# Feed-forward: the rank of the first product's groups, floored to pairs

## The chip, the cores and the metric

The kernel runs on one core of a Trainium2 chip. The metric is the device time of one execution in microseconds (us); the shown time is the median of three runs. Beside it stands one profiled execution, from which all rows below are taken. In the text PE is TensorE (matrix products), PEld its weight loads, DVE VectorE, ACT ScalarE, POOL GpSimd, and SP SyncE, which here only issues DMAs.

## The reference

Hashed attention, then a feed-forward block. Of the attention only this matters here: its output, laid out as `x` with 3072 tokens of 512 features, feeds the block. The block is

```
h = x @ w_in                                              # 3072 x 512 by 512 x 2048
g = h * erf(softplus(h))
y = g @ w_out                                             # 3072 x 2048 by 2048 x 512
```

all in float32 on the chip.

## The kernel before

**Stages.** The attention takes about the first 312 us. Then comes `feed_forward`, the function that the change touches. It works on six tiles of 512 tokens, t = 0 to 5.

**The first product** (`x @ w_in`) of tiles 1 to 5 is done by Winograd's form of Strassen's method at two levels. The outer level makes seven products of half-size blocks, in the order `CHAIN` = P1, P6, P2, P7, P4, P5, P3 (line 1455). Each of them is split once more into seven *groups* in the order `INNER` = Q1, Q5, Q6, Q2, Q7, Q3, Q4 (line 1633). So a tile has 49 groups. A group (`small`, line 1660) is four float32 matmuls of 128x128 by 128x128, which the profile shows as eight MATMUL rows at L1672. Tile 0 has one level only (`plain`, L1433).

**The second product** (`g @ w_out`) is seven products M1 to M7 of eight pieces each (`project`, L1989, four MATMUL rows a piece, 128x256). From the third tile on (t = 2) M4, M7 and M3 are split a second time: seven quarter-block groups in place of eight pieces (`project_small`, L2145, eight MATMUL rows). While tile t runs its first product, the second product of tile t-1 runs beside it; after tile 5's first product only second products are left. The last tile keeps M3 in pieces.

**Accumulators.** A group writes one PSUM bank (`where_of`, L1656): Q1, Q6, Q7 and Q4 share M1 or M2, by turns from one outer product to the next; Q2 uses M4; Q5 and Q3 use M5. After Q1 its bank is copied into M4 by ACT (`seed`, L1449), and Q2 adds to that copy. After each of the other six groups the bank is added to or copied into the hidden block in SBUF (`add_small`: DVE L1702, ACT L1699). The next group of the same bank has to wait for that read. In INNER the groups of the shared bank stand two places apart.

**Weights.** The blocks of `w_in` and their precomputed sums lie in DRAM and come through a ring of two buffers: `load_wi` (L1641, issued by SP) loads the seven operands of an outer product when the outer product two before it has run its last group. The sums of `x` (`presum_xi`, L1654) are made by POOL.

**The gate.** Each hidden block of 128x1024 is put through six ACT instructions (L1821 once, L1829 four times, L1846 once) and three DVE instructions (L1835 twice, L1850 once), which alternate. Sums of gated blocks for the second product are DVE's (L1908 and, for quarter blocks, L2120). The last of them for the last tile stand ahead of M5 and M6 of that tile.

**Who sets the order.** Nothing of this order is written out by hand. Every step is an `Op` with a name, an engine, a cost, a rank, the steps that it comes after, and the ring room it takes. `by_need` (L187) plays the engines against each other with the costs and writes one order for each. On PE the step with the lowest `(rank, name)` is taken among those that could start at that moment (`place`, L240). On the other engines it is the step that is due first, where due times are counted back from PE's order. It plays 5 rounds for each of 3 margins and keeps the order whose PE ends first. The engines then follow that order, and semaphores hold them where a step is late.

The two products are two chains on PE, "P" and "M" (`pe`, L1388): within one, each step comes after the one before, so the rank decides only how the two are interleaved. The ranks before: group g of outer product i of tile t has

```
rank = (0, t + (i + g / 7) / 7)
```

that is, t + (7i + g)/49. A piece or quarter group of the second product of tile t-1 has t + 0.04 + n/56, where n counts the steps in the script (53 a tile with quarter blocks, 56 without). The step of the first is 1/49 = 0.0204, of the second 1/56 = 0.0179.

Of the kernel before, what the change touches and what calls it, by code (L numbers as in the profile page):

```python
# [294 lines left out]
def kernel(  # L295
# [1045 lines left out]
    def feed_forward(pools, check, late):  # L1341
# [27 lines left out]
        def op(name, engine, cost, rank, fn, args, reads=(), writes=(), after=(), **more):  # L1369

            needs = set(after)
            for x in tuple(reads) + tuple(writes):
                if x in wrote:
                    needs.add(wrote[x])
            for x in writes:
                needs |= read.get(x, set())
            for x in reads:
                read.setdefault(x, set()).add(name)
            for x in writes:
                wrote[x] = name  # L1380
                read[x] = set()
            needs.discard(name)
            more.setdefault("late", dict(PE=0.4, DVE=0.3, ACT=0.3, POOL=0.35, SP=0.3)[engine])
            ops.append(
                Op(name, engine, cost, rank, lambda: fn(*args), after=tuple(sorted(needs, key=str)), **more)
            )

        def pe(chain, name, cost, rank, fn, args, **more):  # L1388
            after = more.pop("after", ())
            if last[chain]:  # L1390
                after += (last[chain],)
            last[chain] = name
            op(name, "PE", cost, rank, fn, args, after=after, **more)
# [4 lines left out]
        def part(t, q, fl, tl=None):  # L1398
            room = homes[t][q]
            if tl is None:  # L1400
                return tuple(("h", room, fl, n) for n in range(2))
            return (("h", room, fl, tl),)
# [5 lines left out]
        def xkey(t, name):  # L1408
            key = XKEY[name]
            return key + (t % 2,) if key[0] == "x" else key  # L1410
# [226 lines left out]
        def number(t, i):  # L1637
            return (t if again else t - 1) * 7 + i
# [17 lines left out]
        def where_of(t, i, q):  # L1656
            n = number(t, i) % 2
            return (("M1", "M2")[n]) if q in ("Q1", "Q6", "Q7", "Q4") else dict(Q2="M4").get(q, "M5")
# [23 lines left out]
        def seeded(t, i):  # L1682
            return number(t, i) > 0

        def fresh_of(t, i, q):
            return q in ("Q2" if seeded(t, i) else "Q1", "Q6", "Q5", "Q4")
# [24 lines left out]
        def load_ops(t, i):  # L1711
            n = number(t, i)
            op(
                ("load_wi", t, i),
                "SP",
                0.1,
                (1, t + (i - 1.6) / 7, 0),
                load_wi,
                (t, i),
                reads=(("wi", CHAIN[i], 0), ("wi", CHAIN[i], 1)),  # L1720
                writes=(("ring", n % 2),)
                + (tuple(("w", name, n) for name in ("P1", "P2", "P4", "P7")) if n < 2 else ()),
                late=12.0 if (t, i) == (1, 0) else 8.5,
                far=True,
            )

        def chain_ops(t):
            for i, name in enumerate(CHAIN):
                n = number(t, i)
                into, base = TARGET[name]  # L1730
                load_ops(t, i)
                op(
                    ("presum_xi", t, i),
                    "POOL",
                    1.9,
                    (1, t + (i - 1.5) / 7 if t > 1 or i > 2 else (0.55, 0.6, 0.9)[i], 1),
                    presum_xi,
                    (t, i),
                    writes=(xkey(t, name), ("inn", n % 3)),
                    port=True,  # L1740
                )
                for g, q in enumerate(INNER):
                    rank = (0, t + (i + g / 7) / 7)
                    where = where_of(t, i, q)
                    fl, tl = dict(
                        Q1=(0, 0), Q2=(0, 0), Q6=(0, 1), Q3=(0, 1), Q5=(1, 1), Q7=(1, 1), Q4=(1, 0)
                    )[q]
                    pe(
                        "P",
                        ("small", t, i, q),  # L1750
                        0.875,
                        rank,
                        small,
                        (t, i, q),
                        reads=(xkey(t, name), ("inn", n % 3), ("ring", n % 2)),
                        writes=(("bank", where),),
                    )
                    if q == "Q1" and seeded(t, i):
                        op(
                            ("seed", t, i),  # L1760
                            "ACT",
                            0.51,
                            rank,
                            seed,
                            (where, "M4"),
                            reads=(("bank", where),),
                            writes=(("bank", "M4"),),
                        )
                        continue
                    fresh = fresh_of(t, i, q)  # L1770
                    copy = fresh and base is None
                    target = (("s2", fl, tl),) if into is None else part(t, into, fl, tl)
                    op(
                        ("add_small", t, i, q),
                        "ACT" if copy else "DVE",
                        0.51 if copy else 0.61,
                        rank,
                        add_small,
                        (t, i, q),
                        reads=(("bank", where),) + (part(t, base, fl, tl) if fresh and base is not None else ()),  # L1780
                        writes=target,
                    )
                if name == "P5":
                    for fl in range(2):
                        both = (("s2", fl, 0), ("s2", fl, 1))
                        op(
                            ("add_far", t, fl),
                            "POOL",
                            0.87,
                            (0, t + 6 / 7, fl),  # L1790
                            add_far,
                            (t, fl),
                            reads=both,
                            writes=part(t, 3, fl),
                            late=7.0,
                            far=True,
                        )
                        op(
                            ("add_both", t, fl),
                            "DVE",  # L1800
                            1.16,
                            (0, t + 6 / 7, fl),
                            add_both,
                            (t, fl),
                            reads=both,
                            writes=part(t, 1, fl),
                            port=True,
                        )
# [601 lines left out]
        if again:  # L2410
            load_x(0)
            for k in range(4):
                presum_x(0, k)
            chain_ops(0)
        else:
            if late:
                for k in range(3, 7):
                    name = ("P5", "P6", "P7", "P3")[k - 3]
                    reads = {4: (("w", "P5", 1),), 6: (("w", "P6", 1),)}.get(k, ())
                    op(  # L2420
                        ("late", k), "DVE", 1.16, (1, 0.2, k), late, (k,), port=True,
                        reads=reads, writes=(("w", name, 1),), after=(("late", k - 1) if k > 3 else ("complete", 0, 0),),
                    )
            plain_ops()
            inner_ops()
            presum_w_ops()
        for q in (0, 2, 3, 1):
            gate_ops(0, q)
        for t in range(1, NTILE + 1):
            rest = second_ops(t - 1)  # L2430
            if t < NTILE:
                x_ops(t)
                chain_ops(t)
                for q in (0, 2, 3, 1):
                    gate_ops(t, q)
            rest()
# [143 lines left out]
```

## Time and profile before

| | us |
|---|---|
| median of 3 runs (lowest, highest) | 873.22 (872.52, 875.36) |
| the profiled execution, its own time | 873.12 |
| its span, first to last instruction | 871.3 |
| PE busy | 864.3 |
| DVE busy | 748.9 |
| ACT busy | 638.3 |
| first group of tile 1 starts | 365.24 |
| last group of tile 5 starts | 812.51 |
| last instruction of PE ends | 866.87 |

All times in rows are us from the start of the span; a mean or a minimum in ns is marked. A timeline row gives start, length, engine, line, operation, what is written and read, the shape, and the number of instructions merged in it; in brackets is the idle time of that engine just before, and what ended it. A MATMUL row's length runs past the start of the next one, since matmuls are pipelined: what a group costs PE is the distance from its start to the start of the next. A row cut by the edge of a window shows fewer instructions.

Two facts of the code help in reading it: the output of all groups of the first product reads `M<-area,w_in_sb` or `M<-i,w_in_sb` at L1672; the second product's pieces read `w_out_sb` or `wt` at L1989; quarter groups are at L2145.

### The profile page before, as it was taken

The page shows a single profiled execution, that of the slowest core. Times are in us where ns is not written, and L with a number is a line of the kernel's source. Part 1 is how long each engine was busy: PE and PEld are TensorE (multiplying, and loading weights), DVE is VectorE, ACT ScalarE, POOL GpSimd, SP SyncE. Part 2 cuts the span into 40 slices and gives each one's busy share as a digit, 9 for nine tenths or more (in the row PEclk, how much of TensorE's full clock was granted, in tenths as well). Part 3 has the DMA queues.
Part 4 walks back from the last instruction along what each step waited for, and adds up shares of the span by engine and source line. Part 5 has one row for each costly group of instructions (what it writes and reads, how often), then busy time and mean ns, then how long its engine had stood idle before and what let it go on. Part 6 is the DMA issues. An engine that isn't in the chain of part 4 may idle for free.

```text
span 871.3 us, 15275 instructions
## 1 busy us (share of the span) xinstructions
PE 864.3 (99%) x5992; PEld 671.1 (77%) x5992; DVE 748.9 (86%) x926; ACT 638.3 (73%) x895; POOL 210.5 (24%) x274
## 2 busy tenths in 40 slices
PE   9999999999999999999999999999999999999997
PEld 5444544444454468898999999999999999999997
DVE  5999999999899799789996877699779979898982
ACT  6888888887888757796589457845777586858840
POOL 1111111111111000425241453226632433210000
PEclk9999999999999999999999999999999999999999
DMA  9566866556662246685564647545486657655311
GB/s 223 153 183 193 221 196 181 174 148 171 180 176 103 87 158 219 219 316 203 191 167 162 228 136 226 180 153 201 132 274 235 205 146 229 219 170 164 102 63 41
DMA packets 99825, 155.30 MB, mean 178 GB/s; under 512 B 35182, under 2 KB 48542, under 8 KB 98848
## 3 DMA queue, kind: packets, MB, share of 16 engines
q1 hardware_dynamic: 90112, 120.96, 44.6%
q0 software_dynamic: 9184, 32.81, 12.4%
q8 instruction: 49, 0.80, 0.4%
q10 hardware_dynamic: 448, 0.46, 0.2%
q14 instruction: 32, 0.26, 0.1%
HBM read 119.50 MB, written 29.46 MB: 171 GB/s over the span
## 4 chain that ended last, share of the span: by engine, by line
PE 96%; DVE 1%; DMA 1%; ACT 1%; issue 0%; DVEq 0%
PE M L1672 24%; PE M L1989 23%; PE st L687 18%; PE av L772 15%; PE M L1433 6%; PE M L2145 5%; PE X L2145 3%; PE bits L975 1%; DMA w_in_sb<-wi_P 1%; PE bits L816 1%; PE warm L936 1%; DVE area L1908 0%; PE X L1989 0%; DVE h L1850 0%; DVE e L1835 0%
## 5 line engine op out<-in xcount | busy, mean ns | idle before, releaser
L687 PE MATMUL st<-q,k 64*128 64x384 f32 x768 | 155.1, 482 | 0.0
L1672 PE MATMUL M<-area,w_in_sb 128*128 128x128 f32 x1120 | 146.6, 275 | 1.4 <-DVE h L1702 1.2
L1672 PEld LDWEIGHTS M<-area,w_in_sb 128*128 128x128 f32 x1120 | 142.2, 192 | 6.4 <-DVE h L1702 1.6
L1835 DVE SCALAR_TENSOR_TENSOR e<-w,e 128x1024 f32<-128x1024 f32 x96 | 125.1, 1303 | 19.8 <-ACT w L1829 19.5
L1702 DVE TENSOR_TENSOR h<-M,h 128x512 f32<-128x512 f32 x161 | 108.4, 685 | 33.2 <-PE M L1672 29.3
L1989 PE MATMUL M<-w_out_sb,h 128*128 128x256 f32 x528 | 130.7, 380 | 0.0
L1829 ACT ACTIVATE w<-h,cq 128x1024 f32<-128x1024 f32 x96 | 109.7, 1142 | 22.1 <-DVE e L1835 22.1
L1829 ACT ACTIVATE w<-w,cq 128x1024 f32<-128x1024 f32 x96 | 110.3, 1149 | 1.8
L1672 PEld LDWEIGHTS M<-i,w_in_sb 128*128 128x128 f32 x840 | 107.9, 192 | 3.9
L1672 PE MATMUL M<-i,w_in_sb 128*128 128x128 f32 x840 | 110.4, 275 | 0.0
L1989 PEld LDWEIGHTS M<-w_out_sb,h 128*128 128x128 f32 x528 | 92.8, 191 | 8.5
L1989 PE MATMUL M<-wt,area 128*128 128x256 f32 x384 | 96.3, 380 | 0.0
L687 PEld LDWEIGHTS st<-q,k 64*128 64x128 f32 x768 | 68.5, 187 | 35.8 <-issue 34.4
L760 DVE TENSOR_TENSOR area<-area 128x1536 f32<-128x1536 f32 (+1 forms) x46 | 79.2, 1721 | 6.9 <-ACT area L714 5.7
L1654 POOL TENSOR_TENSOR i<-area,i 128x128 f32<-128x128 f32 x70 | 46.3, 682 | 139.2 <-PE M L1672 138.2
L1821 ACT ACTIVATE e<-h,cq 128x1024 f32<-128x1024 f32 x48 | 54.9, 1145 | 33.8 <-DVE h L1702 22.0
L714 ACT ACTIVATE e_even<-st 128x768 f32<-128x768 f32 x96 | 73.9, 819 | 0.4 <-PE st L687 0.3
L714 ACT ACTIVATE area<-st 128x768 f32<-128x768 f32 x90 | 72.7, 811 | 0.3 <-PE st L687 0.3
L1989 PEld LDWEIGHTS M<-wt,area 128*128 128x128 f32 x384 | 66.9, 191 | 6.0 <-DVE area L1908 0.2
L1850 DVE TENSOR_TENSOR h<-h,e 128x1024 f32<-128x1024 f32 x48 | 61.0, 1270 | 9.5 <-ACT e L1846 9.4
L772 PE MATMUL av<-e_even,v 128*64 128x385 f32 x384 | 65.7, 490 | 0.0
L687 PE MATMUL st<-both 64*128 64x384 bf16 x384 | 63.0, 323 | 0.2 <-ACT e_even L714 0.2
(187 smaller groups left out, 1325.4 us busy)
## 6 DMA issues: line engine op xcount, KB each, us to landing
w_in_sb<-wi_P SPq DMA_DIRECT2D x35, 1792.0 KB
raw<-in_w_out_dram POOLq DMA_DIRECT2D x16, 512.0 KB, 4.3
raw<-in_w_in_dram POOLq DMA_DIRECT2D x14, 512.0 KB, 5.6
v<-in_v_dram SPq DMA_DIRECT2D x32, 192.0 KB
out_dram<-area SPq DMA_DIRECT2D x23, 256.0 KB
q<-in_qkT_dram SPq DMA_DIRECT2D x30, 192.0 KB
k<-in_qkT_dram SPq DMA_DIRECT2D x30, 192.0 KB
r<-rd SPq DMA_DIRECT2D x30, 192.0 KB
```

The lines of the kernel that those rows point to most:

```text
L687: nc.tensor.matmul(out=st[:, ab, 0:HS], lhsT=d["k" + src][rows, keys], rhs=d["q" + src][rows, cols], start=(part == 0), stop=(part == 1),)
L714: nc.scalar.activation(out=e[:, :, 0:HS], in_=st[:, :, 0:HS], func=AF.Exp, scale=scale)
L760: nc.vector.tensor_tensor(out=into, in0=one, in1=two, op=ALU.add)
L772: nc.tensor.matmul(out=d["av", half][rows, 0:w], lhsT=d["v"][:, g * GC + c, rows], rhs=e[:, ab, 0:w], start=(g == 0 and c == 0), stop=(g = ...
L1672: nc.tensor.matmul(out=out_[:, c, :], lhsT=ring[:, W_AT[q], n % 2, c * P : (c + 1) * P], rhs=x, start=((q in ("Q1", "Q5") or q == "Q2" and ...
L1702: nc.vector.tensor_tensor(out=out_, in0=bank_, in1=one, op=ALU.add)
L1821: nc.scalar.activation(out=s, in_=unit(t, q, fl), func=AF.Sigmoid, bias=cq[:, 0:1])
L1829: nc.scalar.activation(out=st["q", t, q, fl, j], in_=f, func=func, scale=scale, bias=cq[:, column : column + 1])
L1835: nc.vector.scalar_tensor_tensor(out=s, in0=st.pop(("q", t, q, fl, j)), scalar=GATE_S[j][1], in1=s, op0=ALU.add, op1=ALU.mult,)
L1850: nc.vector.tensor_tensor(out=h, in0=h, in1=st.pop(("s", t, q, fl)), op=ALU.mult)
L1989: nc.tensor.matmul(out=where[:, sub, :], lhsT=a[:, j // G, j % G, sub * P : (sub + 1) * P], rhs=b[:, j, :], start=first, stop=end, skip_gr ...
L2145: nc.tensor.matmul(out=where[:, n * P : n * P + P], lhsT=a[:, j, :], rhs=b[:, j, :], start=(q in ("Q1", "Q2") and j == 0), stop=(q in ("Q4 ...
```

## The change

One line: the position of the group within the tile, 7i + g, is rounded down to an even number before it becomes the rank.

```
 for g, q in enumerate(INNER):
-    rank = (0, t + (i + g / 7) / 7)
+    rank = (0, t + (7 * i + g - (7 * i + g) % 2) / 49)
     where = where_of(t, i, q)
```

So positions 0 and 1 share a rank, 2 and 3, and so on; position 48, the last of a tile, stands alone. The same rank goes to the group's reader (`seed` or `add_small`), where it counts only after the due time. No step is added or removed, no bank, cost, shape or dependency is altered, and the order within the P chain and within the M chain stays as it is. What changes is the interleaving of the two chains on PE, and through the due times the order that `by_need` writes for DVE, ACT, POOL and SP. An outer product with even i starts a pair with Q1: (Q1 Q5)(Q6 Q2)(Q7 Q3)(Q4, and Q1 of the next). One with odd i starts within a pair: Q1 there, then (Q5 Q6)(Q2 Q7)(Q3 Q4).

## Prediction

> **What bounds the kernel now.** I read the page first, then PE's waits, then the busy times by stage. The page and the waits:
>
> ```profile
> span 871.3 us, 15275 instructions
> ...
> PE 864.3 (99%) x5992; PEld 671.1 (77%) x5992; DVE 748.9 (86%) x926; ACT 638.3 (73%) x895; POOL 210.5 (24%) x274
> ```
> ```profile
> engine line waited for: us in total, times, longest us
> PE M L1672 <- DVE h L1702: 1.2, 1, 1.2
> PE warm L936 <- DVE ones L351: 1.0, 1, 1.0
> PE M L1672 <- DMA w_in_sb<-wi_P: 0.2, 1, 0.2
> PE st L687 <- ACT e_even L714: 0.2, 1, 0.2
> ```
>
> PE is busy for 864.3 of 871.3 us, and in the whole span it waits four times. Two of these waits lie in the stage that the change touches, both ahead of a group of the first product (L1672). A busy PE need not be a fast one, so the distances between starts count more than the 99%. By stage, one window for each of tiles 1 to 5 of the first product:
>
> ```profile
> core 0: us, PE busy (x) PEld busy (x) DVE busy (x) ACT busy (x) POOL busy (x), PEclk, DMA share, GB/s
> 365.00:454.00 89.00, 87.80 (x595) 82.08 (x595) 79.11 (x84) 67.16 (x73) 35.56 (x41) 1.00 0.67 229
> 454.00:546.00 92.00, 92.00 (x618) 86.23 (x617) 70.59 (x73) 63.70 (x71) 34.08 (x40) 1.00 0.56 183
> 546.00:638.00 92.00, 92.00 (x696) 88.39 (x695) 75.47 (x83) 58.22 (x73) 43.43 (x46) 1.00 0.56 178
> 638.00:729.00 91.00, 91.00 (x698) 87.70 (x698) 79.85 (x95) 65.27 (x81) 30.85 (x34) 1.00 0.65 211
> 729.00:814.00 85.00, 84.76 (x637) 81.22 (x636) 73.40 (x90) 66.22 (x79) 13.20 (x20) 1.00 0.57 184
> ```
>
> PE idles 1.20 us in the first window and 0.24 us in the last, nowhere else; its clock is granted in full (1.00) in all five. DVE is the next engine, 79.11 of 89 us (89%) in the first window and 79.85 of 91 (88%) in the fourth. What the steps cost PE is read from PE's timeline:
>
> ```profile
> 560.11 1.05 PE L1672 MATMUL M<-area,w_in_sb 128*128 128x128 f32 x8
> 561.00 1.03 PE L1989 MATMUL M<-w_out_sb,h 128*128 128x256 f32 x4
> 561.87 1.05 PE L1672 MATMUL M<-i,w_in_sb 128*128 128x128 f32 x8
> 562.76 1.03 PE L1989 MATMUL M<-w_out_sb,h 128*128 128x256 f32 x4
> 563.62 1.05 PE L1672 MATMUL M<-i,w_in_sb 128*128 128x128 f32 x8
> 564.52 1.06 PE L1672 MATMUL M<-area,w_in_sb 128*128 128x128 f32 x8
> ```
>
> A group of the first product (P) costs 0.89 us from its start to the next start, whether a piece of the second (M) follows (560.11 to 561.00) or another group (563.62 to 564.52: 0.90). A piece costs 0.86 to 0.87. So PE works at one pace whatever the interleaving, and only its waits can move.
>
> **What the change does to PE's pace.** The same groups and pieces run, in another mixture: mostly P P M M where it was P M P M. A pair's ranks lie 2/49 = 0.0408 apart, the M steps 1/56 = 0.0179, so 2.29 of them fall between two pairs: two, and every third or fourth time three. The rows above already hold both neighbourhoods, and they differ by 0.01 us at most, the last digit shown. There are 245 groups:
>
> ```profile
> L1672 PE MATMUL M<-area,w_in_sb 128*128 128x128 f32 x1120 | 146.6, 275 | 1.4 <-DVE h L1702 1.2
> ...
> L1672 PE MATMUL M<-i,w_in_sb 128*128 128x128 f32 x840 | 110.4, 275 | 0.0
> ```
>
> (1120 + 840)/8 = 245, so at most 122 new neighbourhoods, and 122 x 0.01 bounds the term at -1.2 to +1.2 us. I take 0, because the digit rounds either way.
>
> **What it does to the waits for readers.** The groups of the shared bank (Q1, Q6, Q7, Q4) stand two places apart in P. Before, Q6 M Q2 M Q7: 0.89 + 2 x 0.865 = 2.62 us of other work between Q6's end of issue and Q7. After, an even outer product gives Q6 Q2 M M Q7, an odd one Q6 M M Q2 Q7: the same 2.62 us. With a group's length of 1.05 and its pace of 0.89 the reader has 0.89 + 2.62 - 1.05 = 2.46 us. Two distances shrink from five steps to four, 3.5 us, and stay the longer ones: Q1 to Q2 in an even outer product (through the seed), and Q3 to the next Q5 from an odd to an even one. So no reader is given a shorter time than the shortest of before. What is new is that readers come in twos, 0.89 us apart, and then not for 2.6. In an odd outer product the first of the pair (Q5, Q2, Q3) is not urgent and the second (Q6, Q7, Q4) is; if the first goes first, the second starts later by one add. An add, and the wait that the trace has:
>
> ```profile
> 406.99 1.36 DVE L1908 TENSOR_TENSOR area<-h,h 128x1024 f32<-128x1024 f32 x1
> 408.28 1.48 DVE L1908 TENSOR_TENSOR h<-h,h 128x1024 f32<-128x1024 f32 x1
> 409.86 0.69 DVE L1702 TENSOR_TENSOR h<-M,h 128x512 f32<-128x512 f32 x1
> ```
> ```profile
> 405.71 3.69 PE L1989 MATMUL M<-wt,area 128*128 128x256 f32 x16
> 410.60 1.16 PE L1672 MATMUL M<-area,w_in_sb 128*128 128x128 f32 x8 [1.20 <-DVE h L1702]
> 411.74 2.86 PE L1989 MATMUL M<-wt,area 128*128 128x256 f32 x12
> 414.43 0.83 PE L1672 MATMUL M<-area,w_in_sb 128*128 128x128 f32 x6
> ```
>
> The add takes 0.69 us, so DVE may come 2.46 - 0.69 = 1.77 us late for nothing: more than any one of the long steps quoted (1.48), also more than two adds (1.38), less than a long step and an add (2.17). At 409 two long sums stood ahead of it. That wait cost PE more than its 1.20 us: the 16 rows from 405.71 would have ended their issue at 405.71 + 4 x 0.865 = 409.17, the group began at 410.60 (1.43 lost), took 1.14 to the next start in place of 0.89 (0.25), and the next 12 took 2.69 in place of 2.60 (0.09): 1.77 us in all. The change rewrites the order in which this came about, so the term lies between -1.77 (gone) and +1.77 (a second one like it, priced by that row); I take 0, since the window is unchanged and DVE's load with it.
>
> **What it does to the weights' ring.** The other wait:
>
> ```profile
> 730.20 1.32 SPq L1641 DMA_DIRECT2D w_in_sb<-wi_P  x1
> ```
> ```profile
> 738.67 1.05 PE L1672 MATMUL M<-i,w_in_sb 128*128 128x128 f32 x8
> 739.97 1.16 PE L1672 MATMUL M<-area,w_in_sb 128*128 128x128 f32 x8 [0.24 <-DMA w_in_sb<-wi_P]
> 740.96 1.06 PE L1672 MATMUL M<-i,w_in_sb 128*128 128x128 f32 x8
> ```
>
> Issued at 730.20, the weights let the group go at 739.97: 9.8 us. It lost 1.30 - 0.89 = 0.41 us, and the group after it 0.99 - 0.89 = 0.10: 0.51. From the last group of an outer product, which frees the room, to the first group of the one after next there are seven groups and some eight M steps in both orders, 7 x 0.89 + 8 x 0.865 = 13.2 us, so the load has 3.4 to spare where M work is at hand. At 738 it was not: groups followed each other. The term is -0.51 to +0.51, taken at 0.
>
> **What it does to the end.** The last group of a tile has position 48, which is even: its rank is unmoved. So the first product should still end near 813.4, with the same M work ahead of it. Behind it only the second product is left, and it needs the last tile's gated blocks in time:
>
> ```profile
> 837.25 1.06 ACT L1846 ACTIVATE e<-e 128x1024 f32<-128x1024 f32 x1 [0.75 <-DVE e L1835]
> ```
> ```profile
> 841.12 1.22 DVE L1908 TENSOR_TENSOR area<-h,h 128x1024 f32<-128x1024 f32 x1
> ```
> ```profile
> 839.73 7.93 PE L1989 MATMUL M<-wt,area 128*128 128x256 f32 x36
> ```
>
> The sum that ends at 842.34 is read by M5's second half, 16 rows after 839.73, which is at 839.73 + 16 x 0.216 = 843.19. That leaves 0.85 us, and no other work is there to go first. A gate that ends earlier gains nothing; one that ends later by more than 0.85 us lengthens the kernel one for one. By these rows the term is 0 to +3.7 (below), taken at 0.
>
> **The sum**: 0 + 0 + 0 + 0 on the profiled execution's 873.12 (span 871.3 and 1.8 around it; the median is 873.22): **873.1 us**. The most that can be won from the waits is 1.77 + 0.51 = 2.28 us. A measurement of this kernel can tell some 0.3%, 2.6 us, from no change.
>
> **Rivals.**
>
> *The last gates come late (slower).* The plan of DVE and ACT is written anew from the new due times, over all tiles at once. The end is where a slip has no cover: gate steps alternate between ACT and DVE (ACT at 837.25 waited 0.75 for DVE), and one step of each is 1.06 + 1.22 = 2.28 us. One such turn given away to another block makes M5 wait 2.28 - 0.85 = 1.4 us, two make it 4.56 - 0.85 = 3.7: 876.8. It decides from a slip of 0.85 + 2.6 = 3.5 us. For it: 0.85 us is thin, and the planner's costs (1.16 for the sum) are a little below the rows (1.22 to 1.48). Against it: the end of the first product is not moved, and before the change the same planner left no wait there.
>
> *Adds come late in the chain (slower).* More waits like that at 409, now in odd outer products, where an add stands ahead of the urgent one (0.69 + 1.48 = 2.17 against 1.77). One such late add costs 0.4 us, one behind two long steps 1.77. Three odd outer products a tile with two urgent places each, five tiles: 30 places. It decides from two full waits beyond those of before (3.5 us): 876.7. For it: DVE at 88 to 89% in two windows. Against it: three windows in which DVE is 77 to 86% busy and PE waits for it nowhere.
>
> *Both waits go (a little faster).* 873.1 - 2.3 = 870.8, which is 0.27% and stays inside the 0.3%; with the pace's -1.2 it would be 869.6. For it: both waits arose where the mixture was uneven (four M steps or several groups in a row), and ranks in pairs spread differently. Against it: they follow from what DVE and the load queue had to do.
>
> *The weight loads are the bound (much faster or nothing).* PEld is busy 82.08, 86.23, 88.39, 87.70 and 81.22 us in the five windows, so 23.4 us of them are idle in all. If a mixture could close these gaps the time would be 849.7. Against it: a piece keeps its 0.86 us on either side of a group, and the idle share is that of the long pieces, whose number stays. The Trainium skill (Perfetto Trace Analysis, Identifying the Most-Contended Engine) says that matmul busy time is a poor measure of headroom and that weight-load busy share and achieved FLOPs should be used. By that rule those gaps would be headroom; the distances between starts in this trace do not show any that depends on the order.
>
> *The order hardly changes.* If banks held the second group of each pair back, PE would take an M step first and the old mixture would return: 873.1. The pairs' banks differ, so I give it little.
>
> **How the numbers follow.** Forecast as worked 0.50; order hardly changed 0.04; both waits gone 0.15, of which 0.05 passes 0.3% with the help of the pace; weight loads 0.01; last gates late 0.17; adds late 0.13, these two from the point where they decide. So faster 0.06, same 0.64, slower 0.30. The range reaches down to 870.6 (both waits gone, some of the pace) and up to 877.4 (either slower case at its price, with 0.6 more): about 0.06 is left out below and 0.12 above.
>
> **What would show it.** In PE's timeline groups should merge in twos (x16 rows of L1672) with two or three M steps between, each still 0.89 apart. The wait table of PE should name one to three waits in the five windows, 3 us or less. The ring's distance should stay near 13 us and the last group near 812.5. It is wrong if PE idles over 2.6 us more than before, in the windows (adds late) or between 826 and 847 (gates late), or if a pair's second group keeps another distance than 0.89.

## The result, and the profile after

The changed kernel takes 880.47 us (median of five runs, 879.19 to 881.39), the kernel before 873.22 (872.52 to 875.36, now also five runs). The ratio is 1.008, with a 95% interval of 1.0069 to 1.0092: slower by some 7 us, 3 us above the top of the predicted range. The profiled execution of the changed kernel took 879.19 us; its page:

```profile
span 877.4 us, 15263 instructions
...
PE 865.5 (99%) x5992; PEld 670.7 (76%) x5992; DVE 744.5 (85%) x926; ACT 637.6 (73%) x895; POOL 214.0 (24%) x274
```

The span is 6.1 us longer (877.4 - 871.3) and PE is busy 1.2 us more. So most of the loss, 4.9 us, is time in which PE is not busy. Its table of waits:

```profile
engine line waited for: us in total, times, longest us
PE M L1989 <- DVE area L1908: 2.6, 1, 2.6
PE M L1672 <- DMA w_in_sb<-wi_P: 1.8, 1, 1.8
PE M L1672 <- DVE h L1702: 1.7, 1, 1.7
PE warm L936 <- DVE ones L351: 1.0, 1, 1.0
PE X L2145 <- DVE area L2163: 0.2, 1, 0.2
PE st L687 <- ACT e_even L714: 0.2, 1, 0.2
```

Four waits stand in the changed stage, 6.3 us in all, where there were two of 1.4. The windows of the five tiles tell where:

```profile
core 0: us, PE busy (x) PEld busy (x) DVE busy (x) ACT busy (x) POOL busy (x), PEclk, DMA share, GB/s
365.00:454.00 89.00, 84.66 (x575) 78.80 (x574) 74.20 (x80) 61.82 (x67) 35.25 (x42) 1.00 0.66 225
454.00:546.00 92.00, 92.00 (x618) 86.22 (x617) 70.53 (x75) 64.67 (x72) 39.47 (x40) 1.00 0.55 181
546.00:638.00 92.00, 92.00 (x685) 88.08 (x684) 73.00 (x81) 61.30 (x75) 46.07 (x46) 1.00 0.56 180
638.00:729.00 91.00, 91.00 (x698) 87.70 (x697) 79.38 (x94) 63.23 (x79) 26.35 (x35) 1.00 0.64 212
729.00:814.00 85.00, 83.23 (x631) 79.64 (x630) 73.70 (x88) 64.81 (x78) 14.48 (x20) 1.00 0.57 179
```

In tile 1 PE is busy 3.14 us less than before (87.80 - 84.66), in tile 5 1.53 us less (84.76 - 83.23), and in tiles 2, 3 and 4 it has no gap at all, in either kernel. Before, DVE was busy 79.11 us in the first window, and now 74.20: PE waits for DVE there, and yet DVE does less. So DVE itself is held up by something.

**The pace.** The pairs are there, and they cost what single groups cost:

```profile
470.97 1.06 PE L1672 MATMUL M<-area,w_in_sb 128*128 128x128 f32 x8
471.86 1.89 PE L1989 MATMUL M<-w_out_sb,h 128*128 128x256 f32 x8
473.59 1.95 PE L1672 MATMUL M<-i,w_in_sb 128*128 128x128 f32 x16
475.37 1.03 PE L1989 MATMUL M<-w_out_sb,h 128*128 128x256 f32 x4
```

A group alone keeps 0.89 us to the next start (470.97 to 471.86), a pair 1.78 (473.59 to 475.37), two pieces 1.73. In the five tiles PE's order holds 103 runs of two groups where it held 26, and 14 runs of one where it held 175. If each distance between starts is compared with that pace (112 ns for a row of 128 columns, 216 ns for one of 256), the excess in tile 1 between 395 and 415 is 5.16 us (before 1.78), at tile 5's weights 2.03 (0.50), and at a few small places some 0.8. Tile 1 also started 0.47 us later (365.71 against 365.24), ahead of the changed groups; **no_b** and **no_far** below, which keep all orders of the changed kernel, start it at 365.19 and 364.90, so this part is not the pairs'. 3.4 + 1.5 + 0.8 + 0.47 = 6.2, near the 6.1 between the spans.

**Tile 1.** PE's timeline, where it stops (a group waits for DVE's add, then M5 for DVE's sum):

```profile
405.40 2.32 PE L1672 MATMUL M<-i,w_in_sb 128*128 128x128 f32 x16 [1.67 <-DVE h L1702]
407.56 1.06 PE L1672 MATMUL M<-area,w_in_sb 128*128 128x128 f32 x8
411.26 1.97 PE L1989 MATMUL M<-wt,area 128*128 128x256 f32 x8 [2.64 <-DVE area L1908]
```

DVE, just before:

```profile
392.65 0.68 DVE L1702 TENSOR_TENSOR h<-M,h 128x512 f32<-128x512 f32 x1
397.02 0.69 DVE L1534 TENSOR_TENSOR wt<-area 128x512 f32<-128x512 f32 x1 [3.68 <-DMA wi_P<-wt]
397.74 0.69 DVE L1534 TENSOR_TENSOR wt<-wt,area 128x512 f32<-128x512 f32 x1
398.35 0.68 DVE L1702 TENSOR_TENSOR h<-M,h 128x512 f32<-128x512 f32 x1
398.95 3.49 DVE L1835 SCALAR_TENSOR_TENSOR e<-w,e 128x1024 f32<-128x1024 f32 x2
```

In this trace DVE idles 3.68 us ahead of a sum of weights (L1534, `presum_inner`), with an add and the gate queued behind it in its order. It waits for a DMA: POOL stores the four sums of P5 to DRAM (L1537, `keep_inner`), and the next sums go into the same staging buffer. No such wait is in the trace of before. POOL's timeline, changed kernel first, then the kernel before:

```profile
385.43 1.86 POOL L1654 TENSOR_TENSOR i<-area,i 128x128 f32<-128x128 f32 x2 [5.71 <-PE M L1672]
387.24 0.57 POOL L1537 DMA_DIRECT2D wi_P<-wt  x1
```
```profile
380.95 0.57 POOL L1537 DMA_DIRECT2D wi_P<-wt  x1 [4.10 <-DVE wt L1534]
381.54 1.35 POOL L1654 TENSOR_TENSOR area<-area 128x128 f32<-128x128 f32 x1
```

The store is issued 6.29 us later. In the new order DVE makes the last of these sums 4.17 us later (384.14 against 379.97), and POOL has the store behind two sums of `x` (L1654) that first wait 5.71 us for PE. Then it also takes longer. The views of DMA issues of both kernels, with the KB and the time to landing as last columns (changed kernel first):

```profile
wi_P<-wt POOLq DMA_DIRECT2D x1, 1024.0 KB, 9.8
```
```profile
wi_P<-wt POOLq DMA_DIRECT2D x1, 1024.0 KB, 4.2
```

4.2 us before, 9.8 now. SP's timeline of the changed kernel says with what it flies:

```profile
385.31 0.52 SPq L1641 DMA_DIRECT2D w_in_sb<-wi_P  x1
385.87 0.65 SPq L436 DMA_DIRECT2D area<-xs  x1
```

A load of 1792 KB and one of 1024 KB were issued 1.9 and 1.4 us ahead of it. Before, the store at 380.95 was issued 5.8 us behind a load and had landed at 385.15, before SP issued its next load (386.57). The trace also shows where the time went: in the changed kernel the store moved nothing until 391.6, 4.4 us after its issue, while SP's queue moved 1.30 MB (387.3 to 391.5); before, its first packet moved 1.1 us after its issue. The planner reckons 5.0 us for it in either place (the `late` of the `keep` step).

**Tile 5's weights.** The other place, in PE's, SP's and POOL's timelines of the changed kernel:

```profile
730.19 1.06 PE L1672 MATMUL M<-i,w_in_sb 128*128 128x128 f32 x8
733.01 1.16 PE L1672 MATMUL M<-area,w_in_sb 128*128 128x128 f32 x8 [1.77 <-DMA w_in_sb<-wi_P]
```
```profile
716.15 0.32 SPq L2083 DMA_DIRECT2D w_in_sb<-wm_M  x1
716.56 0.38 SPq L2083 DMA_DIRECT2D b<-wm_M  x1
717.94 13.86 SPq L1641 DMA_DIRECT2D w_in_sb<-wi_P  x2
```
```profile
718.31 0.88 POOL L1709 DMA_DIRECT2D h<-area  x1
722.84 0.87 POOL L1709 DMA_DIRECT2D h<-area  x1
```

The row at 717.94 holds two loads; the second was issued some 13 us later and does not matter here. The first, issued at 717.94, lets PE go only at 733.01, 15.1 us later. M3's sums of weights (768 KB, L2083) were issued 1.8 us ahead of it, and both DMAs by which POOL adds a quarter block (512 KB each, L1709) after it. In the kernel before, the sums were 3.5 us ahead (712.28 to 715.82), one adding DMA 1.4 us ahead (714.42) and one 0.9 us behind (716.71), and the load was in time. The planner reckons 8.5 us for such a load (`late` of `load_wi`).

### The profile page after: what moved, and what is told of

It is laid out like the page before. It is cut to its first block, busy times and chain, and to the rows that moved or that the text cites. A ratio compares the mean times of both kernels' runs of the same rounds, so it can differ in the third digit from the quotient of the medians.

```text
span 877.4 us, 15263 instructions
## 1 busy us (share of the span) xinstructions
PE 865.5 (99%) x5992; PEld 670.7 (76%) x5992; DVE 744.5 (85%) x926; ACT 637.6 (73%) x895; POOL 214.0 (24%) x274
## 4 chain that ended last, share of the span: by engine, by line
PE 93%; DMA 3%; DVE 3%; issue 1%; POOL 0%; ACT 0%; DVEq 0%; POOLq 0%
PE M L1672 23%; PE M L1989 22%; PE st L687 18%; PE av L772 14%; PE M L1433 6%; PE M L2145 4%; PE X L2145 2%; DMA w_in_sb<-wi_P 2%; PE bits L975 1%; DMA wi_P<-wt 1%; PE bits L816 1%; DVE h L1850 1%; DVE e L1835 1%; PE warm L936 1%; PE X L1989 0%
## 5 line engine op out<-in xcount | busy, mean ns | idle before, releaser
L1672 PE MATMUL M<-area,w_in_sb 128*128 128x128 f32 x1120 | 142.9, 275 | 1.8 <-DMA w_in_sb<-wi_P 1.8
L1835 DVE SCALAR_TENSOR_TENSOR e<-w,e 128x1024 f32<-128x1024 f32 x96 | 122.7, 1279 | 24.4 <-ACT w L1829 23.6
L1672 PEld LDWEIGHTS M<-area,w_in_sb 128*128 128x128 f32 x1120 | 137.8, 192 | 5.1 <-DMA w_in_sb<-wi_P 2.0
L1989 PE MATMUL M<-w_out_sb,h 128*128 128x256 f32 x528 | 126.1, 379 | 0.0
L1672 PEld LDWEIGHTS M<-i,w_in_sb 128*128 128x128 f32 x840 | 104.4, 192 | 4.6 <-POOL area L1654 2.0
L1989 PEld LDWEIGHTS M<-w_out_sb,h 128*128 128x128 f32 x528 | 95.0, 191 | 10.0
L1989 PE MATMUL M<-wt,area 128*128 128x256 f32 x384 | 94.5, 380 | 2.6 <-DVE area L1908 2.6
L1654 POOL TENSOR_TENSOR i<-area,i 128x128 f32<-128x128 f32 x70 | 54.0, 791 | 148.7 <-PE M L1672 147.8
L1846 ACT ACTIVATE e<-e 128x1024 f32<-128x1024 f32 x48 | 50.6, 1056 | 19.5 <-DVE e L1835 19.5
```

The source lines that it names most:

```text
L1654: nc.gpsimd.tensor_tensor(out=out_, in0=one_, in1=two_, op=op_)
L1672: nc.tensor.matmul(out=out_[:, c, :], lhsT=ring[:, W_AT[q], n % 2, c * P : (c + 1) * P], rhs=x, start=((q in ("Q1", "Q5") or q == "Q2" and ...
L1835: nc.vector.scalar_tensor_tensor(out=s, in0=st.pop(("q", t, q, fl, j)), scalar=GATE_S[j][1], in1=s, op0=ALU.add, op1=ALU.mult,)
L1989: nc.tensor.matmul(out=where[:, sub, :], lhsT=a[:, j // G, j % G, sub * P : (sub + 1) * P], rhs=b[:, j, :], start=first, stop=end, skip_gr ...
```

## The experiments

Two theories stood first. One (Q in the expectations): the pairs on PE cost nothing, and the loss comes from the orders that the planner wrote for the other engines. The other (R): the pairs on PE cost the time, because readers come in twos. Every ratio below is against runs of the kernel before on the same chip (873.2 to 873.4).

### Half the plan from each kernel

**pe_pairs_only** keeps all orders of before and only brings the groups of a pair together on PE, where the dependencies let it (113 runs of two). The core of the edit, after the planner:

```
+if late:
+    pe_order = [x for x in listed if x.engine == "PE"]
...
+            one, two = (("small", t_, m // 7, INNER[m % 7]) for m in (n_ - 1, n_))
...
+            trial.insert(a + 1, trial.pop(b))
+            if ordered(trial, listed):
+                pe_order = trial
...
+    listed = ordered(pe_order, listed)
```

> PE's order is paired as in the changed kernel (113 pairs of groups), DVE, ACT, POOL and SP keep the orders of the kernel before. Theory Q (the loss comes from the orders that the planner writes for the other queues, above all the DMA of the kept sums that POOL issues later in tile 1): 873 to 875 us, no DVE wait for wi_P<-wt, PE waits of 1 to 3 us in the first product. Theory R (pairs themselves: two readers come at once and the adds fall late): 879 to 881 us, PE waits of some 6 us behind L1702.

**pe_single_others_paired** is the opposite: PE in the order of before, DVE, ACT, POOL and SP in that of the changed kernel.

```
-listed = by_need(ops, dict(e=2, w=2), dict(DVE=3.4) if late else None)
+listed = merged(planned(False), planned(True)) if late else planned(False)
```

> The reverse: PE's order of the kernel before, the other four engines in the orders of the changed kernel. Theory Q: 878 to 882 us, with DVE's wait for the DMA wi_P<-wt (about 3.7 us) and PE's waits near 400 to 412 us still there. Theory R: 873 to 875 us, no such waits on PE.

Measured: 883.65 us, ratio 1.0117 [1.0098, 1.0136], and 895.65, ratio 1.0251 [1.0233, 1.027]. Both lie above what either theory said; the first is nearer to R's figure, the second to Q's. In the first PE waits 4.4 us at once for an add of DVE (at 410.56), and DVE has no wait for the store; in the second DVE has it (4.2 us), but PE waits 14 times in the changed stage, 7.2 us for adds and 4.0 for seeds among them. An order of one engine that was written for another order of PE does not fit it. So these mixtures decide nothing between Q and R, save that the wait for the store comes with the other engines' orders.

### Pairs in some tiles only

Here the planner writes all orders, and only the rank differs. **pairs_tile1** has pairs in tile 1, where most of the loss was:

```
-rank = (0, t + (i + g / 7) / 7)
+rank = (0, t + (7*i + g - ((7*i + g) % 2 if t == 1 else 0)) / 49)
```

> Ranks floored to pairs in tile 1 alone; the planner writes everything anew, and here it puts the DMA of P5's kept sums ahead of the sums of x of the fifth outer product on POOL, as before the change. Theory Q: tile 1 loses at most 2.5 us on PE against 1.8 before, the whole takes 872 to 875 us. Theory R: tile 1 loses some 5 us as in the changed kernel, the whole takes 876 to 878 us.

**pairs_rest** has them in tiles 2 to 5 (`if t > 1`):

> Ranks floored to pairs in tiles 2 to 5, tile 1 as before the change; planned anew. Theory Q: tile 1 loses about what it did before (1 to 2.5 us), behind it a wait for the weights near 730 us of at most 2 us: 873 to 876 us. Theory R: the pairs of four tiles cost more than those of one, 877 us or more.

Measured: pairs_tile1 872.76 us (ten runs), ratio 0.999 [0.998, 1.0]; pairs_rest 875.35 (six runs), ratio 1.0032 [1.0019, 1.0044]. With pairs in tile 1 and their own plan, that tile loses some 1.3 us where the changed kernel loses 5.16. Its store of P5 is issued at 380.69 and lands in 4.4 us, and DVE does not wait for it. So R falls for tile 1: with a plan of their own, paired readers there do not make DVE late. PE's waits for pairs_rest, whose time is 2.0 us more than that of before:

```profile
PE M L1672 <- DMA w_in_sb<-wi_P: 1.9, 1, 1.9
PE M L1672 <- DVE h L1702: 1.0, 1, 1.0
```

It has the wait for tile 5's weights, and in tile 1 a wait of 1.0 us where the kernel before had 1.2.

### The store in tile 1

**keep_early** is the changed kernel with two steps moved in its list: DVE's last sum of P5 right behind the one ahead of it, and POOL's store behind that.

```
+(("inner", "P5", 3), ("inner", "P5", 2)),
+(("keep", "P5"), ("inner", "P5", 3)),
```

> The changed kernel with two steps moved: the last sum of P5's weights behind the third on DVE, and its DMA behind it on POOL, ahead of the waiting sums of x; PE's and ACT's orders are the changed kernel's. Theory Q: DVE's wait of 3.7 us for wi_P<-wt falls under 1 us, PE's waits in tile 1 fall by about 3.4 us, the whole takes 876 to 878 us; what is left over 873 is the wait for the weights at 731 us and the small ones behind it. Theory R: 879 to 881 us, since the pairs stay.

**told** leaves the order to the planner but gives it the landing that the trace shows in company:

```
                     after=behind(name, False),
-                    late=5.0,
+                    late=10.0,
```

> The changed kernel, with the planner told that the kept sums' DMA takes 10.0 us to land where it had 5.0 (the trace has 9.8 for the one that DVE waits for); everything is planned anew. Theory Q (the loss in tile 1 comes from a plan that counts on that DMA too early): no DVE wait for wi_P<-wt, PE loses at most 2.5 us in tile 1, the whole takes 873 to 877 us. Theory R (pairs): 879 to 881 us.

Measured: keep_early 878.72 us, 1.0067 [1.0042, 1.0092]; told 877.63, 1.0048 [1.0031, 1.0065]. In both DVE's wait is gone; the store lands in 4.5 and 4.7 us. In told it is issued at 386.45, only 0.8 us earlier than in the changed kernel, but 5.8 us behind SP's last load and ahead of the next: there it is the company that has changed, hardly the moment. (Its plan is another one throughout: tile 1 starts at 370.76.) Tile 1's excess falls from 5.16 to 2.87 and to 3.3 us, not to the 1.8 of before. So both fall short of what Q expected: PE's waits in tile 1 fall by 2.05 us in keep_early, not by 3.4, and told loses more than 2.5 us there and lies 0.6 us above 877. PE's waits for keep_early:

```profile
PE M L1989 <- DVE area L1908: 2.3, 1, 2.3
PE M L1672 <- DMA w_in_sb<-wi_P: 2.0, 1, 2.0
```

The first of PE's two waits in tile 1 is gone, but M5 still waits for its sum, and the weights of tile 5 are untouched. The four runs of keep_early also fall in two pairs: 877.25 and 877.12 at a mean granted clock of 1.000, 880.22 and 880.19 at 0.995. A mean lower by 0.005 over 878 us is some 4 us of full clock, so the clock can account for the 3 us between them; the expectation of 876 to 878 is met by the first pair only. At clock 1.000 the changed kernel took 879.19 (one run), keep_early 877.2 (two) and told 876.3 (one). So the late store, with the late sum ahead of it, is shown to be worth some 2.3 us of tile 1's 3.4 by the distances there, and 2.0 us of the whole. The other 1.1 us is still there with an early store: M5 waits for a sum of DVE, and no run isolates why DVE is behind at that place.

### Tile 5's weights

Two kernels leave one companion of the load out. **no_b** drops the loads of M3's sums of weights in tile 3:

```
 for far, near in pieces_of_b(name):
-    nc.sync.dma_start(out=near, in_=far)
+    if again or (t, name) != (3, "M3"):
+        nc.sync.dma_start(out=near, in_=far)
```

> The changed kernel, all orders kept, without the two DMAs (512 and 256 KB) that load M3's sums of w_out for the fourth tile, issued 1.8 us ahead of the weights for tile 5: those quarter groups read what M7 left there. Theory L (the load of the weights shares the DMA engines with whatever else is under way): the wait of 1.8 us at 731 us falls under 0.5 us, the span by 1.5 to 2 us. Theory O (the weights' load takes its 15 us by itself, or the wait has another cause): the wait stays at 1.5 to 2 us.

**no_far** drops the two adding DMAs of tile 4:

```
-nc.gpsimd.dma_start(out=quarter(t, 3)[:, fl, :, :], in_=S2[:, fl, :, :], accum_op=ALU.add)
+if again or t != 4:
+    nc.gpsimd.dma_start(out=quarter(t, 3)[:, fl, :, :], in_=S2[:, fl, :, :], accum_op=ALU.add)
```

> The changed kernel, all orders kept, without the two adding DMAs of 512 KB in tile 4, so that the hidden block 3 of that tile lacks P5's part. Theory L: the wait at 731 us falls under 0.5 us here too, the span by 1.5 to 2 us. If only the transfers of the same queue (SP's) count, it stays at 1.5 to 2 us here and goes with M3's sums alone. Theory O: it stays in both.

Measured: no_b 879.54 us (two runs), 1.0072 [1.0052, 1.0092]; no_far 878.36 (two runs), 1.0059 [1.0038, 1.0079]. Two runs leave the times wide, and the place itself says more. In no_b the load takes 13.7 us (719.73 to 733.44) and the group still waits 0.40 us (excess 0.66 instead of 2.03). Its span of 877.7 us is no shorter than the changed kernel's, against the expectation: tile 1 lost some 2.3 us more in that run, most of it at a low clock (last section). Without the adding DMAs the span is 1.9 us shorter and the group does not wait, as PE's timeline shows (the edit moves later lines by one):

```profile
729.98 1.06 PE L1672 MATMUL M<-i,w_in_sb 128*128 128x128 f32 x8
730.88 1.06 PE L1672 MATMUL M<-area,w_in_sb 128*128 128x128 f32 x8
731.77 1.06 PE L2146 MATMUL M<-w_in_sb,h 128*128 128x128 f32 x8
```

0.90 and 0.89 us between starts. No packet of any queue starts between 728 and 731 in that trace, so the same load, issued at 717.73, has landed in at most 10.3 us where it took 15.1. The adding DMAs are on POOL's queue, the load on SP's: these transfers delay the load across queues, not by standing in line. (M3's loads stand ahead of it on its own queue; for them the run does not tell the two apart.) The Trainium skill (DMA: Bandwidth & Descriptors, Issuing engines are not separate DMA queues) says that all engines' DMAs run on the same 16 DMA engines and interleave there; no_far agrees, with 15.1 us against at most 10.3.

**rest_no_far** is pairs_rest without these two DMAs:

```
-rank = (0, t + (i + g / 7) / 7)
+rank = (0, t + (7*i + g - ((7*i + g) % 2 if t > 1 else 0)) / 49)
...
+if again or t != 4:
```

> Pairs in tiles 2 to 5 with all orders of that kernel, without the two adding DMAs of tile 4 (its hidden block 3 lacks P5's part). Theory L: what these pairs cost is the wait for tile 5's first weights, which share the DMA engines with those two; the wait of 1.9 us at 727 us is gone and the whole takes 872.8 to 873.8 us. Theory R (the pairs cost in many small places): 875 us as with the DMAs.

873.47 us (ten runs), ratio 0.9998 [0.9986, 1.001]. The 2.0 us that pairs_rest loses were that one wait: with it gone, pairs in four tiles are no slower than none.

### The wait that was there before

The prediction priced the wait at 409 at 1.77 us. **add_first** is the kernel before with the awaited add moved ahead of the two long sums on DVE; **pairs_tile1_add_first** is pairs_tile1 with the same move and one of the long sums (`presum_g` 0, 0, 1) put ahead of the other. In both the add overwrites a block of tile 0 before a sum of M6 has read it, so that sum has other values; the time is still that of this order.

```
+(("add_small", 1, 3, "Q6"), ("gate", 0, 1, 1)),
```

> The kernel before, with one add of tile 1 (Q6 of P7) moved on DVE ahead of the two long sums at 407 to 410 us. By the prediction's price that wait costs 1.77 us: 871.4 to 872.0 us, and no PE wait behind L1702. If the sums then come late for M5 instead, PE waits there and the time stays at 873.

> Pairs in tile 1 alone, with the same add moved ahead, and the first sum behind it ahead of the other: the waits of tile 1 (1.3 us in that kernel's run) should nearly go: 871.4 to 872.2 us against 872.8.

add_first: 873.17 us (twelve runs), 0.9996 [0.9987, 1.0006]. The group no longer waits, but M5 does, 1.4 us, until DVE's third sum behind the moved add ends at 412.12. At this place DVE is behind with its work: with the add first, a sum makes PE wait instead. pairs_tile1_add_first: 872.3 (twelve runs), 0.9983 [0.9974, 0.9992]; there 0.3 us of wait is left, and the time lies 0.1 us above what was expected.

### A version with pairs that is not slower

**pairs_23** has pairs in tiles 2 and 3 only (`if 1 < t < 4`) and leaves nothing out. (The "20 of 49 places" in its expectation is a slip: two of the five tiles are meant.)

> Pairs in tiles 2 and 3 alone, planned anew, result complete. Theory L and Q: neither the kept sums of tile 1 nor the weights of tile 5 are touched by pairs, so the time is that of the kernel before within its waits, 872.5 to 874.5 us. Theory R: 20 of 49 places of the changed kernel's pairs are in these tiles, so some 40% of its 7 us: 875.5 to 876.5 us.

872.42 us (ten runs, 871.53 to 873.28), ratio 0.9982 [0.997, 0.9993]. The only wait left in the stage:

```profile
PE M L1672 <- DVE h L1702: 1.0, 1, 1.0
```

It is the fastest complete version here, by 0.18%, which is less than the 0.3% named in the prediction; its interval excludes no change, if barely.

## Why the prediction was wrong

**Pace: right.** Taken at 0; pairs keep 0.89 us a group. In tiles 2, 3 and 4 PE has no gap.

**Waits for readers: the step that failed.** It gave -1.77 to +1.77 and took 0, "since the window is unchanged and DVE's load with it". The first half held where it was tried: pairs_tile1 shows that the readers' time suffices in tile 1. The second half looked at how much DVE has to do, not at what DVE waits for. The term measured +3.4 us. Some 2.3 of it is shown to come from a DMA that POOL issued late and that then landed late; the cause of the other 1.1 stays open. The prediction itself said that the whole plan is written anew, and used that only for the end of the stage; POOL's queue was not walked through. Its own sign of being wrong was met: PE idles 4.7 us more than before in the five windows, where 2.6 was the limit.

**Ring of weights: the other step that failed.** It took 9.8 us, one load's landing, as a constant and so found 3.4 us to spare. The distance was near what it said: from the issue at 717.94 to the start of the wait, 733.01 - 1.77 = 731.24, are 13.3 us, against 13.2 worked out. But the load took 15.1. no_far shows what it left out, the transfers under way beside the load: without two of them the same load took at most 10.3. The bound of +0.51 was the wait already seen, and nothing said that another could not be longer; measured, the term is +1.5.

**End: right, nearly.** Taken at 0. The last group starts at 818.11, later than before by the 5.6 us lost ahead of it, and after 814 there is one wait of PE, 0.2 us at 830, for a step of DVE (L2163) that adds up quarter blocks and is no part of the gate; it and the slower steps around it cost 0.5 of the 0.8 us above. *The last gates come late* did not happen.

**The other rivals.** *Adds come late in the chain* named the right engine and sign and gave 876.7. Its cause, paired readers in odd outer products of all tiles, does not stand beside pairs_tile1 and rest_no_far, which have such pairs in tile 1 and in tiles 2 to 5 and are no slower: the add was late at one place, where DVE had been held. That its 876.7 lies nearer to the result than the forecast is luck. *Both waits go* did not happen: waits of both kinds are there, at other places and larger. *The weight loads are the bound* and *the order hardly changes* fail with the rows of the pace and the count of pairs.

**A term that was not in the sum.** The profiled execution kept the full clock. The other four runs had a mean granted clock of 0.998 and took 0.8 to 2.2 us more. No term asked what a wait of 2.6 us does to the clock. The sum on the profiled execution is 873.12 + 3.4 + 1.5 + 0.8 + 0.47 = 879.3 (measured 879.19). The median of 880.5 belongs to the runs with the lower clock; these have no trace, so where their clock was low is not shown.

## What to carry to other kernels

A rank on the busiest engine rewrites the order of every queue that is planned from it, so price such a change by walking the other queues too: which DMA now stands behind a step that waits, and which transfers now start together. A DMA's landing time is not a property of the DMA; take it from rows with the company that it will have, and compare that with the planner's constant. And try a change of order stage by stage: here the same pairs cost 7 us in all five tiles, 2 us in tiles 2 to 5, and nothing in tile 1 alone or in tiles 2 and 3.

## What the runs showed of the hardware

**The same transfer, up to twice the time.** The store of 1024 KB took 4.2 us when the last load had been issued 5.8 us ahead of it, and 9.8 us when 2816 KB of loads had been issued within 2 us ahead of it; 4.4 of these passed before its first packet moved. The load of tile 5's weights (1792 KB) took 15.1 us beside 768 KB of loads and two adding DMAs of 512 KB, 13.7 without these loads, and at most 10.3 without the adding DMAs. Another load of this size, at 730 in the kernel before, took 9.8.

**A wait of 1.6 to 2.6 us can halve PE's clock, and need not.** The changed kernel and no_b have the same wait of 2.64 us in tile 1. The granted clock (the column behind POOL) in the 3.7 us after it, changed kernel first:

```profile
411.30:415.00 3.70, 3.70 (x18) 3.29 (x19) 3.70 (x4) 1.50 (x2) 0.12 (x1) 1.00 0.33 133
```
```profile
411.30:415.00 3.70, 3.63 (x10) 2.91 (x11) 3.70 (x4) 1.62 (x2) 0.24 (x1) 0.57 0.35 144
```

18 rows against 10 in the same time; the 16 rows that the wait held back took 3.69 us and 5.38. In no_far the clock had already fallen to 0.63 between 408 and 411, after a wait of 1.60 us that ended at 405.19 (and one of 0.47 six us earlier), and in pe_pairs_only it is 0.50 for the 4 us after a wait of 4.45. So a short wait can be paid for twice; the two pairs of runs of keep_early, 3 us apart, would fit that, but the slower two have no trace. The Trainium skill (TensorE: Matmul & The Clock Gate, Part 1) says that the clock falls after about one idle window of 3.4 us, and that the window runs freely, so that the moment varies from run to run. The variation agrees with these runs; the length does not quite, since here waits shorter than that were enough.

**Two multiplies of DVE took 3.49 us** at 398.95 in the changed kernel, where one takes 1.30 on average over the kernel before. POOL's sums ran beside the second half of them (from 400.10), but in the kernel before a multiply beside such sums took 1.21, so the cause stays open. This is no difference of the changed kernel: while these sums of POOL (L453) run, some step of DVE is long in the other traces too (2.29 us for a sum, L1908, at 401.00 in the kernel before, 4.08 for the two multiplies in keep_early), and no run leaves them out.
